# Gated attention and token mixer: the first layer's last pass as two passes of one block, and a shorter inner polynomial for gelu

## Chip, cores and metric

One core of one Trainium2 chip runs the whole kernel. The metric is device time in microseconds (us) of one launch.

## The reference

Input x is 2048 rows by 512 columns. Two branches are computed and mixed row by row:

```python
g = sigmoid((x * gate_w).sum(-1))
a = softmax attention of x, 32 heads of 16, then @ wo
h = layernorm(x)                                  # (2048, 512)
u = gelu(einsum("bsd,sf->bdf", h, w1) + b1)       # f = 1792: the first layer, over rows
y = einsum("bdf,fs->bds", u, w2) + b2             # the second layer, back to rows
out = g * a + (1 - g) * transpose(y)
```

gelu is the tanh form, 0.5 u (1 + tanh(0.798 (u + 0.0447 u^3))). The change touches the first layer of the second branch and its gelu.

## The kernel before

Values are kept as pairs of a high part (fp32r) and the low rest, so each product is three matmuls on TensorE (PE): high by high, high by low, low by high. To split a weight, ScalarE (ACT) copies the high part and GpSimd (POOL) subtracts it for the low part.

The work runs in stages: the values, keys and queries of attention are projected; then the first layer; then attention, in 128 parts, with the second layer and the late queries on PE beside it; then the output.

**The first layer.** The 1792 columns of w1 are taken in passes of up to NB = 512: four blocks of 128 columns in each of the first three passes, two blocks in the last (256 columns). Each pass runs over the 16 row blocks of x (`for at, c in enumerate(cs)`); a block has a PSUM bank of its own in which its 16 x 3 matmuls are added up (`layer`, L420). The last pass takes row blocks 8 to 15 first and 0 to 7 after (`order`, L126). The weights come through a queue, `blocks`: `load_weight` (L135) issues the next load into one of four raw tiles, `split_weight` (L149) splits the oldest that is loaded into one of three pairs of tiles `w_hi`, `w_lo`, and `weight` (L157) does both and hands out the oldest pair. Three pairs are split ahead of the loop, so a call of `weight` splits the weight three places on, whose tile is the one that the matmuls of this call's weight read. Behind the blocks of w1, the same queue holds those of w2: four 128 x 128 blocks in one tile.

**gelu.** `gelu` (L428) is a generator of seven steps for one block of 128 columns by 512: bias add on VectorE (DVE), Square on ACT, the inner polynomial on DVE (L437 and L438), tanh on ACT (L440), the outer product on DVE (L442), the high part on ACT (L444) and the low part on DVE (L446). The blocks of one pass go through it in the next pass. In the first and the last pass the order on ACT, DVE and POOL is written out by hand (`manual_schedule`): row block by row block, first the weight's split, then the steps that are due. In the last pass (L523) the four blocks of the pass before begin at row blocks 0, 1, 7 and 8, a step for each row block. In the two passes between, the compiler orders these engines.

**The last two blocks.** They have no pass behind them. Their bias add (L549, `late_u`) stands between the first layer and attention; the rest of their gelu lies in the first parts of attention, on DVE but for the tanh (L553 to L574): square (L555), the polynomial in two operations (L559, L563), tanh on ACT (L566), outer product (L570) and split. The tables `amid` and `later` say in which part, and whether ahead of the part's last two DVE copies or at its end.

**Attention.** A part computes 16 score tiles (L1067) of 128 x 512 on PE, each in a bank of its own while seven banks last. ACT takes ten of them out as exponentials (six single ones, L1093, and two pairs, L1031); DVE copies the other six (L1089), and ACT then takes the exponential of these six at once (L1102). PE applies them to the values (L963), with one or several matmuls of the dense layers beside the scores (L1076). All five engines have a written order here.

Of the kernel before, what the change touches and what calls it, by code (L numbers as in the profile page):

```python
# [13 lines left out]
AF = mybir.ActivationFunctionType  # L14
ALU = mybir.AluOpType
# [8 lines left out]
P = 128  # L24
S = 2048
D = 512
F = 1792
H = 32
DH = 16
NS = S // P  # L30
ND = D // P
NF = F // P
NB = 512
# [4 lines left out]
GELU_A = 0.044715  # L38
# [22 lines left out]
def gated_mix(ctx: ExitStack, tc: tile.TileContext, a_x, a_wqkv, a_wo, b_w1, b_b1, b_w2, b_b2, gate_w, out):  # L61
    nc = tc.nc
# [30 lines left out]
    g = const.tile([P, NS], F32, name="g")  # L93
# [23 lines left out]
    def bank():  # L117
        return acc.tile([P, NB], F32, name="acc")
# [4 lines left out]
    xt_lo = xt_pool.tile([P, ND, S], F32R, name="xt_lo")  # L123


    order = {f0: [(c + (NS // 2 if f0 + NB >= F else 0)) % NS for c in range(NS)] for f0 in range(0, F, NB)}  # L126
    blocks = [b_w1[c * P : (c + 1) * P, f0 : min(f0 + NB, F)] for f0 in order for c in order[f0]]
    blocks += [
        b_w2[c * P : min(c + 4, NF) * P, t * P : (t + 1) * P].rearrange("(k p) s -> p k s", p=P)
        for t in range(NS)  # L130
# [4 lines left out]
    def load_weight():  # L135
        if blocks:
            src = blocks.pop(0)
            raw = wk.tile([P, NB], F32, name="w_raw", bufs=4)
            if len(src.shape) == 2:
                raw = raw[:, : src.shape[1]]  # L140
                dst = raw
            else:
                raw = raw[:, : src.shape[1] * P]
                dst = raw.rearrange("p (k s) -> p k s", s=P)
            with tc.issue_after(x_load.ins):
                nc.sync.dma_start(dst, src)
            loaded.append(raw)
# [9 lines left out]
    def weight():  # L157
        load_weight()
        split_weight()
        return ready.pop(0)  # L160
# [17 lines left out]
    with tc.tile_pool(name="vp", bufs=1, side="right") as pool:  # L178
# [122 lines left out]
        for t in range(2, NS):  # L301
# [9 lines left out]
            ps = bank()  # L311
# [22 lines left out]
    h_hi, h_lo = {}, {}  # L334
# [15 lines left out]
    def ln_load(c):  # L350
        xs[c] = ln_x[:, c % 4, :]
        nc.sync.dma_start(xs[c], xf[c * P : (c + 1) * P, :])
# [10 lines left out]
    if True:  # L363
# [19 lines left out]
        for b in range(ND):  # L383
            wk_b, wq_b = qk_w.pop(0), qk_w.pop(0)
            kmax = bd.tile([P, NQ], F32, name="kmax")
            for at, (n, keys) in enumerate(jobs):
                ps = project(wk_b if keys else wq_b, n)
# [11 lines left out]
                if at in (2, 5):  # L399
                    c = 2 * b + at // 3  # L400
# [16 lines left out]
    u_hi = u_pool.tile([P, NF, D], F32R, name="u_hi")  # L417
    u_lo = u_pool.tile([P, NF, D], F32R, name="u_lo")

    def layer(ps, hi, lo, rhs, first, last):  # L420
        for i, p in list(enumerate(ps))[:: 1 if len(ps) == NB // P else -1]:
            wh, wl = hi[:, i * P : (i + 1) * P], lo[:, i * P : (i + 1) * P]
            for k, (a, b) in enumerate(((wh, rhs[0]), (wh, rhs[1]), (wl, rhs[0]))):
                nc.tensor.matmul(p, a, b, start=first and k == 0, stop=last and k == 2)  # L424

    with tc.tile_pool(name="gl", bufs=2, side="right") as gl:

        def gelu(ps, fb):  # L428

            u = gl.tile([P, D], F32, name="gu")  # L430
            s = gl.tile([P, D], F32, name="gs")
            hi, lo = u_hi[:, fb, :], u_lo[:, fb, :]
            nc.vector.tensor_scalar_add(u, ps, b1[:, fb : fb + 1])
            yield
            nc.scalar.activation(s, u, AF.Square)
            yield
            nc.vector.tensor_scalar(s, s, GELU_A, 1.0, ALU.mult, ALU.add)  # L437
            nc.vector.tensor_mul(s, s, u)  # L438
            yield
            nc.scalar.activation(s, s, AF.Tanh, scale=GELU_C)  # L440
            yield
            nc.vector.scalar_tensor_tensor(u, s, 1.0, u, ALU.add, ALU.mult)  # L442
            yield
            nc.scalar.copy(hi, u)  # L444
            yield
            nc.vector.tensor_tensor(lo, u, hi.bitcast(F32), ALU.subtract)  # L446
            yield

        beside = {mybir.EngineType.Activation, mybir.EngineType.DVE, mybir.EngineType.Pool}
        for c in range(AHEAD):  # L450
            ln_load(NH + c)


        def shift_rows(engine, t):
            for i in range(2):
                engine.memset(t[i * HALF + SHIFT[0] : i * HALF + SHIFT[0] + DH].bitcast(F32), -1.0)

        landed, waiting = [], []

        def stack(dst, src, which, pair, planes):  # L460
            b, r0 = divmod(pair * 2 * DH, P)
            for i in range(2):
                rows = slice(r0 + i * DH, r0 + (i + 1) * DH)
                for row, *part in planes:
                    at = slice(i * HALF + row, i * HALF + row + DH)
                    waiting.append((dst[at].bitcast(F32), src[b][part[which], rows, :]))

        def load_next():
            if waiting:
                landed.append(nc.sync.dma_start(*waiting.pop(0)))  # L470

        def load_all():
            while waiting:
                load_next()

        def load_k(g):
            t = k_bufs[g % 2]
            stack(t, kp_d, 1, g % NP, PAIRS)
            if g:
                load_all()  # L480
            return t

        def load_q(g):
            half, pair = divmod(g, NP)
            t = q_bufs[g % 2]
            stack(t, qp_d[half], 0, pair, [*PAIRS, SHIFT])
            if g:
                load_all()
            return t

        k_bufs, q_bufs = [], []

        def first_loads():
            k_bufs.append(first_stacks.tile([P, S], F32R, name="ks"))
            q_bufs.append(first_stacks.tile([P, QW], F32R, name="qs"))
            shift_rows(nc.vector, k_bufs[0])
            return {0: load_k(0)}, {0: load_q(0)}

        STEPS = 7
        gelus = []  # L500
        for f0, cs in order.items():
            n = min(NB, F - f0) // P
            ps = [bank() for _ in range(n)]
            in_order = f0 == 0 or f0 + NB >= F
            if f0 == NB:
                kt, qt = first_loads()
            if not in_order:
                for step in gelus:
                    list(step)
                gelus = []  # L510
            with tc.manual_schedule(engines=beside) if in_order else ExitStack():
                for at, c in enumerate(cs):
                    hi, lo = weight()

                    if f0 == 0 and AHEAD < c <= NH:
                        ln_load(NH + c - 1)
                    if f0 == 0 and AHEAD < c <= NH + AHEAD:
                        ln_rows(NH + c - AHEAD - 1)
                    layer(ps, hi, lo, (h_hi[c], h_lo[c]), at == 0, at == NS - 1)
                    if at % 2:  # L520
                        load_next()
                    for i, step in enumerate(gelus):
                        if 0 <= at - i // 2 * STEPS - i % 2 < STEPS:  # L523
                            next(step)
            gelus = [gelu(ps[i], f0 // P + i) for i in range(n)]
    h_ctx.close()


# [17 lines left out]
    for i, p in reversed(list(enumerate(ps))):  # L546
        u = out_pool.tile([P, D], F32, name="row", bufs=3)
        at = NF - len(ps) + i
# [136 lines left out]
    calls, later, amid = {}, {}, {}  # L685
# [4 lines left out]
    def on_dve(at, *what):  # L690
        later.setdefault(at, []).append(what)
# [161 lines left out]
            on_dve(2 * at + 2, *finish)  # L853
        return put(steps, at, [len(steps)])

    for i in range(2):
        on_dve(1 + i, tanh, i)
        on_dve(2 + i, outer_parts, i)
    for p, mid, what, i in (
        (0, True, squares, 0),  # L860
        (0, False, cubic, 0),
        (1, True, inner, 0),
        (1, False, squares, 1),
        (1, False, cubic, 1),
        (2, True, inner, 1),
        (2, False, outer, 0),
        (3, True, outer, 1),
    ):
        if mid:
            amid.setdefault(p, []).append((what, i))  # L870
        else:
            later.setdefault(p, []).insert(1 if what is cubic and i else 0, (what, i))
    call(3, load_xt, 2)
    for b in range(ND):
        call(6 + b, nc.sync.dma_start, v_d[b], vb[b][:, :BV])
    at, queries = 0, [(b, n) for n in (2, 3) for b in range(ND)]
    for t in range(NS):
        at = put(second_layer(t), at, [14] * 3)
        if queries:
            b, n = queries.pop(0)  # L880
            at = put_whole(late_query(b, n), at)
# [24 lines left out]
    for t in range(NH):  # L906
        at = put_whole(project(t), at)
# [82 lines left out]
    with tc.manual_schedule(engines=engines):  # L990
# [3 lines left out]
        for p in range(LAST + 1):  # L994
            grp, ph = divmod(p, PHASES)
            second = ph % 2
            if ph == 0:
                sums[grp] = ot_pool.tile([P, NB], F32, name="ot")
                latest["clear"] = nc.gpsimd.memset(sums[grp], 0.0)
                at = [[0, 0], [0, 0]]  # L1000
# [41 lines left out]
            for n in in_turn:  # L1042
                i, qb = head[n], qbs[n]
                c = at[i][qb]
                at[i][qb] += 1
                if n < TWO[0][0]:
                    if n >= BANKS:
                        ones[share[n - BANKS]] = psum.tile([P, NB], F32, name=f"s{share[n - BANKS]}")
                    s = ones[share[n % BANKS]]
                else:  # L1050
# [14 lines left out]
                    s = twos[share[2 if n == NSC - 1 else (n - BANKS) % BANKS]]  # L1065
# [8 lines left out]
                if n < n_b:  # L1074
                    ps, a, b, begin, last, done = beside[n]
# [72 lines left out]
    with (  # L1148
# [16 lines left out]
        sums, hi, lo = (column_halves(x) for x in (whole[:, :NB], parts[:, :NB], parts[:, NB:]))  # L1165
        last = column_halves(last_ot)
# [63 lines left out]
    with tc.If(far_off != 0):  # L1230
        with (
# [6 lines left out]
            for b in range(ND):  # L1238
                with tc.For_i(0, P // DH, 1) as hi:
# [11 lines left out]
                    for t in range(NS):  # L1251
                        s = ps_s.tile([P, S], F32, name="s")
# [6 lines left out]
                        p = pool.tile([P, S], F32, name="p", bufs=1)  # L1259
# [4 lines left out]
                        for n in range(NQ):  # L1264
                            tp = ps_t.tile([P, NB // P, P], F32, name="tp")
                            for i in range(NB // P):
                                c = n * (NB // P) + i
# [3 lines left out]
                            for i in range(NB // P):  # L1271
                                c = n * (NB // P) + i
# [38 lines left out]
```

## Time and profile before

| | us |
|---|---|
| median of 3 runs | 1265.4 (1265.24 to 1265.51) |
| the profiled execution | 1265.31 |
| its span, first to last instruction | 1263.5 |
| busy: PE, PE weight loads | 1254.8, 829.2 |
| busy: DVE, ACT, POOL | 856.7, 1069.0, 198.6 |
| the first layer's matmuls | 122.9 to 277.6 |

In the profile's lines, times are us from the start of the span. A line of the timeline gives start, duration, engine, line of the kernel, operation, what is written from what, shapes, and the count where several equal instructions follow each other; in brackets stands the engine's idle time before it and what ended that. "acc" is the first layer's bank, "gu" and "gs" are gelu's tiles, "row" and "big" those of the late blocks, "s", "t" and "u" score tiles, "p" and "pe" their exponentials. A line of the waits gives who waited for whom: us in total, times, longest. The mean granted clock of the span is 0.999.

### The profile page before, as it was taken

What the parts mean: (1) busy time and instruction counts of PE and PEld (TensorE: products, weight loads), DVE (VectorE), ACT (ScalarE), POOL (GpSimd) and SP (SyncE); (2) the same over time, 40 slices, a digit from 0 to 9 for tenths busy, and PEclk for the clock granted to TensorE, in tenths of its full rate; (3) what the DMA queues carried; (4) which work ended last, traced back from release to release, by engine and by line L of the source; (5) the groups of instructions that cost most, each with busy time, mean ns of one, the idle gap of its engine ahead of it and who ended that gap; (6) DMA issues with size and microseconds to landing.
All of it is one profiled execution on the core that took longest, in us unless ns stands there. A gap on an engine that the chain in (4) does not pass through costs nothing.

```text
span 1263.5 us, 32833 instructions
## 1 busy us (share of the span) xinstructions
PE 1254.8 (99%) x13342; PEld 829.2 (66%) x13342; DVE 856.7 (68%) x1562; ACT 1069.0 (85%) x1405; POOL 198.6 (16%) x316
## 2 busy tenths in 40 slices
PE   9999999999999999999999999999999999999998
PEld 7888888875666666666666666666666666666656
DVE  5675453178767676767677677776777677678883
ACT  4443343269999999999999999999999999999990
POOL 0220444461010101010110101111111111000000
PEclk9999999999999999999999999999999999999999
DMA  4799443244744444544344433444543443366611
GB/s 134 251 340 329 143 122 106 81 127 110 214 121 104 90 102 85 158 86 97 77 105 94 99 90 83 91 87 81 113 101 73 90 100 60 56 166 175 151 60 70
DMA packets 100556, 152.32 MB, mean 121 GB/s; under 512 B 17109, under 2 KB 56171, under 8 KB 96300
## 3 DMA queue, kind: packets, MB, share of 16 engines
q1 hardware_dynamic: 99820, 149.08, 46.0%
q8 instruction: 107, 1.75, 0.6%
q10 hardware_dynamic: 576, 1.05, 0.2%
q14 instruction: 53, 0.43, 0.1%
HBM read 105.39 MB, written 44.68 MB: 119 GB/s over the span
## 4 chain that ended last, share of the span: by engine, by line
PE 96%; DVE 2%; ACT 1%; issue 0%; DVEq 0%
PE av L963 31%; PE s L1067 21%; PE acc L424 12%; PE t L1067 9%; PE acc L75 8%; PE t L963 5%; PE dn L1076 3%; PE u L1067 3%; PE pa L1162 2%; DVE pe L1089 1%; PE acc L199 1%; PE acc L268 0%; DVE ot L985 0%; PE acc L245 0%; ACT p L1093 0%; ACT pe L1102 0%
## 5 line engine op out<-in xcount | busy, mean ns | idle before, releaser
L1093 ACT ACTIVATE p<-s 128x512 f32<-128x512 f32 x768 | 411.9, 789 | 0.1
L1102 ACT ACTIVATE pe<-pe 128x3072 f32<-128x3072 f32 x129 | 380.9, 2954 | 0.0
L1067 PE MATMUL s<-qs,ks 64*128 64x512 f32 x1280 | 329.8, 400 | 0.6 <-ACT p L1093 0.6
L1089 DVE COPY pe<-s 128x512 f32<-128x512 f32 x512 | 323.6, 685 | 5.5 <-PE s L1067 1.5
L1067 PEld LDWEIGHTS s<-qs,ks 64*128 64x128 f32 x1280 | 225.7, 184 | 92.7 <-issue 52.3
L1031 ACT ACTIVATE p<-t 128x1024 f32<-128x1024 f32 x256 | 278.7, 1267 | 0.0
L963 PE MATMUL av<-p,v 128*32 128x256 f32 x3880 | 227.2, 379 | 0.0
L1089 DVE COPY pe<-u 128x512 f32<-128x512 f32 x256 | 164.8, 685 | 67.1 <-PE u L1067 67.1
L963 PE MATMUL av<-pe,v 128*32 128x256 f32 x3072 | 192.5, 383 | 0.0
L985 DVE TENSOR_TENSOR ot<-av,ot 128x512 f32<-128x512 f32 (+2 forms) x160 | 93.0, 582 | 140.9 <-PE av L963 139.6
L68 POOL TENSOR_TENSOR w_lo<-w_raw,w_hi 128x512 fp32r<-128x512 f32 (+1 forms) x128 | 153.0, 1202 | 196.8 <-ACT w_hi L67 99.9
L1076 PE MATMUL dn<-u_lo,w_hi 64*128 64x512 f32 x448 | 181.0, 404 | 0.0
L1076 PE MATMUL dn<-u_hi,w_hi 64*128 64x512 f32 x448 | 180.7, 403 | 0.0
L963 PEld LDWEIGHTS av<-p,v 128*32 128x32 f32 x3880 | 126.0, 110 | 83.3 <-ACT p L1093 0.2
L1076 PE MATMUL dn<-u_hi,w_lo 64*128 64x512 f32 x448 | 180.6, 403 | 0.0
L1067 PE MATMUL t<-qs,ks 64*128 64x512 f32 x512 | 142.5, 413 | 0.0
L963 PEld LDWEIGHTS av<-pe,v 128*32 128x32 f32 x3072 | 86.8, 109 | 80.7 <-ACT p L1093 35.7
L1080 POOL MEMSET token<- 1x1 f32 x128 | 11.3, 88 | 742.7 <-PE dn L1076 679.4
L67 ACT CAST w_hi<-w_raw 128x512 fp32r<-128x512 f32 (+1 forms) x67 | 38.0, 569 | 82.7 <-PE acc L424 63.1
L1067 PEld LDWEIGHTS t<-qs,ks 64*128 64x128 f32 x512 | 73.2, 184 | 50.8 <-ACT p L1093 48.6
L424 PE MATMUL acc<-h_hi,w_hi 128*128 128x512 f32 x224 | 87.9, 392 | 0.0
L424 PE MATMUL acc<-h_hi,w_lo 128*128 128x512 f32 x224 | 87.9, 392 | 0.0
(171 smaller groups left out, 1615.8 us busy)
## 6 DMA issues: line engine op xcount, KB each, us to landing
w_raw<-in_B_w_dram SPq DMA_DIRECT2D x96, 256.0 KB
ks<-kp SPq DMA_DIRECT2D x192, 128.0 KB
qs<-qp SPq DMA_DIRECT2D x256, 64.0 KB
kp<-pc SPq DMA_DIRECT2D x16, 512.0 KB
qp<-pc SPq DMA_DIRECT2D x8, 768.0 KB
qp<-row SPq DMA_DIRECT2D x24, 256.0 KB
v<-v SPq DMA_DIRECT2D x4, 1088.0 KB
x<-in_A_x_dram SPq DMA_DIRECT2D x16, 256.0 KB
```

The lines of the kernel that those rows point to most:

```text
L67: copy(hi, src)
L68: return sub(lo, src, hi.bitcast(F32), ALU.subtract)
L75: nc.tensor.matmul(ps, a, b, start=start and n == 0, stop=stop and n == last)
L424: nc.tensor.matmul(p, a, b, start=first and k == 0, stop=last and k == 2)
L963: mm = nc.tensor.matmul(av[32 * j : 32 * (j + 1), i * QC : (i + 1) * QC], vb[b][:, v_at : v_at + 32], pt[:, h * QC : (h + 1) * QC], start= ...
L985: latest["add"] = nc.vector.tensor_tensor(x, y, x, ALU.add)
L1031: pairs_done.append(nc.scalar.activation(pt, twos[low, low + 1], AF.Exp, scale=SCALE))
L1067: nc.tensor.matmul(s, kt[grp][rows_i, c * P : (c + 1) * P], qt[grp][rows_i, qb * NB : (qb + 1) * NB], start=True, stop=True,)
L1076: mm = nc.tensor.matmul(ps, a[half], b[half], start=begin and not second, stop=last and bool(second))
L1089: nc.vector.tensor_copy(pt, s)
L1093: one = nc.scalar.activation(pt, s, AF.Exp, scale=SCALE)
L1102: done = nc.scalar.activation(x, x, AF.Exp, scale=SCALE)
```

## The change

- The last pass (two blocks) becomes two passes of one block each. A load of weights for these passes holds one block of 128 columns for four row blocks (128 x 512, in the form that w2's loads have), so `weight` is called for each fourth row block only.
- The blocks of the third pass go through gelu beginning at row blocks 0 and 7 of the first short pass and 0 and 8 of the second; the block of the first short pass itself begins at row block 4 of the second. One block, not two, is left for attention; its steps stand in parts 0 to 2.
- Square is scaled by the root of 0.0447, so that one DVE operation, (s + 1) u, replaces the two of the inner polynomial in the twelve, now thirteen, blocks that go through `gelu`.

```diff
+    starts = [0, NB, 2 * NB, F - 2 * P, F - P, F]
+    order = {f0: [(c + (NS // 2 if f0 + NB >= F else 0)) % NS for c in range(NS)] for f0 in starts[:-1]}
+    width = {f0: f1 - f0 for f0, f1 in zip(starts, starts[1:])}
+    blocks = [b_w1[c * P : (c + 1) * P, f0 : f0 + NB] for f0 in order if width[f0] == NB for c in order[f0]]
+    blocks += [
+        b_w1[c * P : (c + 4) * P, f0 : f0 + P].rearrange("(k p) s -> p k s", p=P)
+        for f0 in order
+        if width[f0] == P
+        for c in order[f0][::4]
+    ]
...
-    def layer(ps, hi, lo, rhs, first, last):
-        for i, p in list(enumerate(ps))[:: 1 if len(ps) == NB // P else -1]:
+    def layer(ps, hi, lo, rhs, first, last, n0=0):
+        for i, p in enumerate(ps, n0):
...
-            nc.scalar.activation(s, u, AF.Square)
+            nc.scalar.activation(s, u, AF.Square, scale=GELU_A**0.5)
             yield
-            nc.vector.tensor_scalar(s, s, GELU_A, 1.0, ALU.mult, ALU.add)
-            nc.vector.tensor_mul(s, s, u)
+            nc.vector.scalar_tensor_tensor(s, s, 1.0, u, ALU.add, ALU.mult)
...
-                    hi, lo = weight()
+                    if n > 1 or at % 4 == 0:
+                        hi, lo = weight()
...
-                    layer(ps, hi, lo, (h_hi[c], h_lo[c]), at == 0, at == NS - 1)
+                    layer(ps, hi, lo, (h_hi[c], h_lo[c]), at == 0, at == NS - 1, 0 if n > 1 else at % 4)
...
-                    for i, step in enumerate(gelus):
-                        if 0 <= at - i // 2 * STEPS - i % 2 < STEPS:
+                    for begin, step in gelus:
+                        if 0 <= at - begin < STEPS:
                             next(step)
-            gelus = [gelu(ps[i], f0 // P + i) for i in range(n)]
+            if f0 == F - 2 * P:
+                gelus = [(b - NS, g) for b, g in gelus if b >= NS] + [(4, gelu(ps[0], f0 // P))]
+                gelus.sort(key=lambda x: x[0])
+            else:
+                gelus = [(b, gelu(ps[i], f0 // P + i)) for i, b in zip(range(n), (0, 7, NS, NS + 8))]
...
+    amid[0] = [(squares, 0)]
+    on_dve(0, cubic, 0)
+    amid[1] = [(inner, 0)]
+    on_dve(1, tanh, 0)
+    on_dve(2, outer, 0)
+    on_dve(2, outer_parts, 0)
```

More of the change, by code (lines that the diff above doesn't have):

```diff
@@ L123, in gated_mix @@
     xt_lo = xt_pool.tile([P, ND, S], F32R, name="xt_lo")
-    order = {f0: [(c + (NS // 2 if f0 + NB >= F else 0)) % NS for c in range(NS)] for f0 in range(0, F, NB)}
-    blocks = [b_w1[c * P : (c + 1) * P, f0 : min(f0 + NB, F)] for f0 in order for c in order[f0]]
+    starts = [0, NB, 2 * NB, F - 2 * P, F - P, F]
[8 more added lines that the diff above has]
+    ]
     blocks += [
@@ L501, in gated_mix @@
         for f0, cs in order.items():
-            n = min(NB, F - f0) // P
+            n = width[f0] // P
             ps = [bank() for _ in range(n)]
@@ L507, in gated_mix @@
             if not in_order:
-                for step in gelus:
+                for _, step in gelus:
                     list(step)
@@ L854, in put_whole @@
         return put(steps, at, [len(steps)])
[L856 to L872, printed above, removed]
+    amid[0] = [(squares, 0)]
[4 more added lines that the diff above has]
+    on_dve(2, outer_parts, 0)
     call(3, load_xt, 2)
```

## The prediction

> **What bounds the kernel now.** I read the page first, then the chain of waits in order of time, then what ScalarE (ACT) waits for, then the timelines of ACT, VectorE (DVE) and GpSimd (POOL) around the end of the first layer. The page, ACT's busy tenths in 40 slices of the span, and the chain of waits by engine:
>
> ```profile
> ACT  4443343269999999999999999999999999999990
> ...
> PE 96%; DVE 2%; ACT 1%; issue 0%; DVEq 0%
> ```
>
> By the chain TensorE (PE) looks like the bound of the whole kernel; ACT is full only from the tenth slice on. The chain in order of time, and everything ACT waits for from 277 us to the end:
>
> ```profile
> 122.92 154.68 PE acc L424 x672
> 277.59 0.89 PE s L1067 x2
> 278.76 2.56 ACT p L1093 x5
> ...
> ACT o_sum L1210 <- PE pa L1192: 6.4, 1, 6.4
> ACT e L1180 <- DVE o_sum L1179: 5.2, 1, 5.2
> ACT w_hi L67 <- PE acc L424: 0.7, 1, 0.7
> ```
>
> Two stages with two bounds. The first layer is 672 matmuls in 154.68 us, 0.230 us apart, with no gap: PE bounds it, and the change keeps every one of these matmuls. From the first exponential on, ACT waits for nothing until the two lines of the closing stage (L1180, L1210): attention is one unbroken stream of ACT work. So each microsecond that ACT is given or spared there, and each microsecond by which its stream starts later, should move the end of the kernel by as much. The timeline of ACT:
>
> ```profile
> 277.45 0.62 ACT L67 CAST w_hi<-w_raw 128x512 fp32r<-128x512 f32 x1 [0.74 <-PE acc L424]
> 278.06 3.26 ACT L1093 ACTIVATE p<-s 128x512 f32<-128x512 f32 x6
> 281.16 1.99 ACT L1031 ACTIVATE p<-t 128x1024 f32<-128x1024 f32 x2
> 282.96 2.84 ACT L1102 ACTIVATE pe<-pe 128x3072 f32<-128x3072 f32 x1
> 285.63 3.11 ACT L1093 ACTIVATE p<-s 128x512 f32<-128x512 f32 x6
> ...
> 292.95 0.78 ACT L566 ACTIVATE big<-big 128x512 f32<-128x512 f32 x1
> 293.47 3.20 ACT L1093 ACTIVATE p<-s 128x512 f32<-128x512 f32 x6
> ...
> 308.77 3.24 ACT L1093 ACTIVATE p<-s 128x512 f32<-128x512 f32 x6
> ...
> 316.19 2.26 ACT L1093 ACTIVATE p<-s 128x512 f32<-128x512 f32 x4
> ```
>
> One of the 128 parts of attention is six single exponentials, two pairs and one wide one: 316.19 - 308.77 = 7.42 us when nothing is added. The late tanh of a block (L566; there are two, one a part later) takes a slot of 293.47 - 292.95 = 0.52 us, and the part that holds the first lasts from 285.63 to 293.47, 7.84 us. PE is done with the first layer at 277.45, where it releases the last weight buffer, and the first exponential starts 0.61 us later.
>
> **The change, part by part.** *PE.* The pass over 256 columns becomes two passes over 128, each with 16 x 3 matmuls. Two times 48 is 96 matmuls, as before; the last pass now fills only its second half, from about 277.45 - 11.05 = 266.4 us on. No change in PE time. *Weights.* Instead of 16 loads and splits of 128x256 there are 8 of 128x512. How these fit is seen in the pass before, which has the same 12 matmuls for one 128x512 load:
>
> ```profile
> 244.12 0.62 ACT L67 CAST w_hi<-w_raw 128x512 fp32r<-128x512 f32 x1 [2.18 <-PE acc L424]
> 246.92 0.62 ACT L67 CAST w_hi<-w_raw 128x512 fp32r<-128x512 f32 x1 [2.18 <-PE acc L424]
> ...
> 256.72 0.41 ACT L67 CAST w_hi<-w_raw 128x256 fp32r<-128x256 f32 x1 [0.99 <-PE acc L424]
> 258.12 0.41 ACT L67 CAST w_hi<-w_raw 128x256 fp32r<-128x256 f32 x1 [0.99 <-PE acc L424]
> 258.44 0.63 ACT L435 ACTIVATE gs<-gu 128x512 f32<-128x512 f32 x1
> ```
>
> ACT copies one weight each 246.92 - 244.12 = 2.80 us and idles 2.18 us of them "<-PE": supply is ahead, so larger loads cost PE nothing. If that cover went, a late weight would cost its lateness; none is near. But the rows tell a second thing. The copy is queued on ACT in program order, and it waits until PE has finished the weight three places earlier, whose buffer it takes. Whatever stands behind it on ACT waits too. Before, such a gate opened each 258.12 - 256.72 = 1.40 us, once for each row block, and the gelu steps of that row block stood right behind it (the Square at 258.44). After, it opens once for four row blocks, about each 2.8 us, and gelu steps of four row blocks bunch behind it. In the last pass, from 266.4 to 277.45, the gates open at about 269.2, 272.0, 274.7 and 277.4 us.
>
> *Gelu beside the last pass.* Three blocks must go through it in 11 us (starting at row blocks 0, 4 and 8), where before four went through in 22 us. Prices of the steps, and what DVE and POOL do to each other:
>
> ```profile
> 211.13 0.69 DVE L438 TENSOR_TENSOR gs<-gs,gu 128x512 f32<-128x512 f32 x1
> 212.20 1.66 DVE L438 TENSOR_TENSOR gs<-gs,gu 128x512 f32<-128x512 f32 x1
> 211.92 1.39 POOL L68 TENSOR_TENSOR w_lo<-w_raw,w_hi 128x512 fp32r<-128x512 f32 x1 [1.61 <-ACT w_hi L67]
> 266.74 0.53 POOL L999 MEMSET ot<- 128x512 f32 x1 [0.40 <-PE acc L424]
> 266.81 1.40 DVE L433 TENSOR_SCALAR gu<-acc,b 128x512 f32<-128x512 f32 x2
> ```
>
> A dependent ACT step is 0.63 us, a DVE step 0.69, the bias add 1.40/2 = 0.70. A DVE step that begins while POOL subtracts (212.20, POOL until 213.31) ends 0.55 us after POOL, at 213.86. I take that price: end of POOL plus 0.55. The Trainium skill, page "SBUF — State Buffer", section "Who interferes with whom", says that a DVE instruction with two SBUF inputs and a GpSimd instruction that reads SBUF exclude each other, and that the later one is fully blocked until the first is done. By that rule the blocked step would have ended at 213.31 + 0.69 = 214.0, and each of the blocked steps below would end 0.14 us later than by the row, some 0.5 us in all; the trace agrees with the blocking and is a little kinder, and the sum goes by the row.
>
> Followed from the first gate with these prices (an estimate): copy 269.2, Square 269.7 to 270.4, inner step blocked by POOL's subtraction (269.9 to 271.2) until 271.75, tanh until 272.4, outer step 273.1, add of the second block 273.8, its Square 274.45, low part of the first block behind POOL 275.0, inner 275.7, tanh 276.35, outer 277.05, add of the third block 277.75, its Square 278.35, low part of the second behind POOL 278.9, inner 279.6, tanh 280.25, outer 280.95, cast 281.6, low part up to 282.85 behind POOL's last subtraction. PE is through at 277.45. So on ACT a Square, a tanh, a weight copy and a cast, four slots of about 0.53 us, fall into attention, and on DVE two low parts, an inner and an outer step. Now what stands behind them:
>
> ```profile
> 277.19 1.40 DVE L549 TENSOR_SCALAR row<-acc,b 128x512 f32<-128x512 f32 x2
> 278.52 2.52 DVE L1089 COPY pe<-s 128x512 f32<-128x512 f32 x4
> 280.96 0.68 DVE L555 TENSOR_TENSOR big<-row 128x512 f32<-128x512 f32 x1
> 281.56 1.28 DVE L1089 COPY pe<-u 128x512 f32<-128x512 f32 x2
> ```
>
> The wide exponential of the first part started at 282.96 because DVE's last two copies ended at 281.56 + 1.28 = 282.84: DVE is already tight there. Before, DVE was free for its first copy at 278.52.
>
> If the queues keep the order of the program, the first exponential waits for the cast (281.55 instead of 278.06, +3.5) and DVE's copies for the low part (282.85 to 283.5 instead of 278.52): the wide exponential is 4.3 to 5.0 us late, and the rest of the stream with it. If the compiler mixes the tail with attention by readiness, DVE still owes from 277.75 on a blocked low part until 278.9, then inner, outer, low part (3 x 0.69) and the one late add (0.7): 281.65, 3.1 us past 278.52; POOL's last subtraction can add up to 0.7. The memset at 266.74, which belongs to attention and yet runs between the subtractions of the pass, shows that such mixing happens. What goes the other way: one late block instead of two, so one tanh, -0.52 us on ACT. The DVE steps of that block (square, inner, outer, split) and the shorter inner polynomial in earlier passes come out of DVE time behind which nobody waits: 0, a gain excluded by ACT's unbroken stream. If ACT weren't the bound there, it could be worth up to what the first four parts last over steady ones, (308.77 - 278.06) - 4 x 7.42 = 1.03 us with both tanh in it.
>
> Sum: +3.1 - 0.52 = +2.6 with mixing, +3.8 to +4.5 without. I take +3.0, nearer the mixed end because of that memset row. The profiled execution took 1265.31 us (span 1263.5 and 1.8 around it), 0.09 below the median of the runs, 1265.4: 1265.31 + 3.0 = **1268.3 us**.
>
> **Rivals.** *Order kept (strict queues).* 1265.31 + 3.8 to 4.5, about 1269.5 us. For it: both stages are written as ordered queues. Against it: the memset. It decides if DVE's first copy of attention stands behind the last low part.
>
> *A light tail.* POOL's subtractions happen not to meet the chain: without the four waits behind POOL (about 0.65, 0.5, 0.45 and 0.55 us in the steps above) the last block is through its low part at about 280.7 us. What then falls on DVE is an inner and outer step and a low part, 2.0 us, less 0.52: about 1266.8 us, within the bound of no change. For it: a few tenths in the start of a step decide whether it meets POOL. Against: POOL subtracts 1.4 of each 2.8 us.
>
> *The tail fits (the other side).* The chain of the third block ends before PE does, ACT's stream starts at 278.06 as before, and the spared tanh remains: 1265.31 - 0.52 = 1264.8 us, not slower. The place is the third block's low part, and the point is 277.45: the 17 dependent steps that follow the first gate, 269.2, would have to take under 0.49 us each. Against it: ACT alone takes 0.63, DVE 0.69. For it: only that the scheduler may place steps better than I follow them.
>
> *The blocks gain more than I see.* The change would have to save over 2.5 us of an ACT stream in which only 1.03 us is more than steady work; I find no row for it.
>
> **How the numbers follow.** Forecast 0.40, order kept 0.27, light tail 0.20, tail fits 0.08, more gain 0.05. About 0.2% (2.5 us) is what a measurement of this kernel can tell from no change, so the bound lies at 1267.9. The forecast's own spread, 1267.7 to 1269.0 for starts of steps that differ by some tenths, lies above it for about 0.33 of its 0.40: slower 0.33 + 0.27 = 0.60; same 0.07 + 0.20 + 0.08 = 0.35; faster 0.05. The range 1265.2 to 1270.2 leaves out the two gaining cases (0.13) and some 0.07 of later tails.
>
> **What would show it.** Right: matmuls of L424 still without a gap; gates on ACT 2.8 us apart; a Square, tanh and cast of the first layer's gelu after the last L424 matmul; the wide exponential of the first part starting about 3 us later against the first score matmul than 282.96 - 277.52 = 5.4; ACT's stream then unbroken at 7.42 us a part, and one L566 of 0.52 us. Its row for the score matmul:
>
> ```profile
> 277.52 0.50 PE L1067 MATMUL s<-qs,ks 64*128 64x512 f32 x1
> ```
>
> Wrong: gelu's last low part before 277.45, a gap among the L424 matmuls (then weights, not gelu, cost), a part other than the first one stretched, or a first part as long as before with the end later all the same.

## The result, and the profile after

| | before | after |
|---|---|---|
| median of 7 runs, us | 1265.44 | 1269.57 (1269.2 to 1269.82) |
| ratio, 95% interval | | 1.0031 [1.0019, 1.0042] |
| the profiled execution | 1265.31 | 1269.82 |
| its span | 1263.5 | 1267.9 |

The change costs 4.1 us, 0.31%; the interval of the ratio, 0.19 to 0.42%, reaches down to the prediction's bound of 0.2%. The time lies in the range that was forecast, 1265.2 to 1270.2, and 1.3 us above the forecast of 1268.3; what happened is the rival "order kept", about 1269.5. Three things in the profile after show it. The first is what PE waits for from another engine (us in total, times, longest):

```profile
PE s L1068 <- DVE row L561: 3.9, 1, 3.9
PE acc L253 <- DVE idle L248: 1.2, 1, 1.2
```

The second line stood in before too (L245 there). The first is new: one score matmul waits 3.9 us for the bias add of the late block (L561, `late_u`), which frees that block's PSUM bank. Timeline of PE, around the end of the first layer:

```profile
277.17 0.39 PE L432 MATMUL acc<-h_hi,w_lo 128*128 128x512 f32 x1
277.49 0.49 PE L1068 MATMUL s<-qs,ks 64*128 64x512 f32 x1
...
283.05 0.79 PE L1068 MATMUL s<-qs,ks 64*128 64x512 f32 x1 [3.90 <-DVE row L561]
283.64 0.62 PE L1068 MATMUL s<-qs,ks 64*128 64x512 f32 x1
```

The first score starts at 277.49, before at 277.52: PE's first layer has the same length. Six scores find free banks; the seventh has to take the bank of the block that has just been added up. Timeline of DVE after:

```profile
270.32 1.36 DVE L445 SCALAR_TENSOR_TENSOR gs<-gs,gu 128x512 f32<-128x512 f32 x1 [1.06 <-ACT gs L443]
...
279.77 0.69 DVE L449 SCALAR_TENSOR_TENSOR gu<-gs,gu 128x512 f32<-128x512 f32 x1 [0.69 <-ACT gs L447]
281.14 0.99 DVE L453 TENSOR_TENSOR u_lo<-gu,u_hi 128x512 fp32r<-128x512 f32 x1 [0.68 <-ACT u_hi L451]
282.24 0.75 DVE L561 TENSOR_SCALAR row<-acc,b 128x512 f32<-128x512 f32 x1
282.91 1.88 DVE L1090 COPY pe<-s 128x512 f32<-128x512 f32 x3
```

The late add's input was ready at 277.56 (277.17 + 0.39). It runs at 282.24, straight behind the last low part of the third block's gelu (L453). Its row shows no wait of its own: its place in DVE's queue keeps it. Attention's first copies (L1090) stand behind it, at 282.91, where before had them at 278.52. This is the second thing, and on ACT the same order stands:

```profile
269.13 0.62 ACT L67 CAST w_hi<-w_raw 128x512 fp32r<-128x512 f32 x1 [0.92 <-PE acc L432]
...
272.25 0.60 ACT L67 CAST w_hi<-w_raw 128x512 fp32r<-128x512 f32 x1
...
275.95 0.61 ACT L67 CAST w_hi<-w_raw 128x512 fp32r<-128x512 f32 x1
...
279.64 0.60 ACT L67 CAST w_hi<-w_raw 128x512 fp32r<-128x512 f32 x1
280.50 0.62 ACT L451 CAST u_hi<-gu 128x512 fp32r<-128x512 f32 x1 [0.25 <-DVE gu L449]
281.02 1.57 ACT L1094 ACTIVATE p<-s 128x512 f32<-128x512 f32 x3
...
288.67 2.77 ACT L1103 ACTIVATE pe<-pe 128x3072 f32<-128x3072 f32 x1 [0.73 <-DVE pe L1090]
...
298.67 0.69 ACT L578 ACTIVATE big<-big 128x512 f32<-128x512 f32 x1
...
313.89 3.24 ACT L1094 ACTIVATE p<-s 128x512 f32<-128x512 f32 x6
...
321.30 3.24 ACT L1094 ACTIVATE p<-s 128x512 f32<-128x512 f32 x6
```

The first exponential (281.02) is the first thing behind the last cast. The wide exponential of the first part is 5.71 us late (288.67 against 282.96). From 313.89 on, where before had 308.77, the stream is 5.12 us late at the same 7.41 us a part: 0.59 came back, with one tanh less.

The third thing shows in the windows. Columns: stretch, its length, busy us and count of PE, PEld, DVE, ACT and POOL, PE's granted clock (the share of full speed that PE was given), DMA share, GB/s:

```profile
277.00:279.00 2.00, 2.00 (x15) 1.19 (x13) 1.97 (x3) 1.06 (x2) 0.92 (x1) 1.00 0.58 164
279.00:283.00 4.00, 0.15 (x2) 0.00 (x0) 2.51 (x5) 3.23 (x6) 1.27 (x1) 0.92 1.06 205
283.00:289.00 6.00, 5.95 (x38) 3.73 (x42) 4.79 (x8) 3.84 (x6) 1.99 (x3) 0.50 0.62 82
289.00:291.00 2.00, 2.00 (x32) 1.06 (x26) 0.48 (x2) 2.00 (x1) 1.89 (x1) 0.95 0.00 0
```

After the wait PE runs at half its clock for about 6 us, while the copies and the wide exponential depend on its scores. From the late add to the wide exponential it takes 288.67 - 282.24 = 6.43 us, and from DVE's first copy 288.67 - 282.91 = 5.76 us, where before took 282.96 - 278.52 = 4.44 us.

At the other end of the kernel, the timelines of DVE in before and then in after, with the operation of the last output row:

```profile
1257.33 0.75 DVE L1205 SCALAR_TENSOR_TENSOR base<-pa,g,base 128x512 f32<-128x512 f32 x1 [2.03 <-PE pa L1162]
```

```profile
1262.53 0.75 DVE L1206 SCALAR_TENSOR_TENSOR base<-pa,g,base 128x512 f32<-128x512 f32 x1 [2.03 <-PE pa L1163]
```

The last operation ends 5.2 us later (1263.28 against 1258.08), the span only 4.4: what lies behind it (call it the closing time) fell from 5.4 to 4.6 us. So the sum of after, on the spans, is +4.39 (DVE's first copy, 282.91 against 278.52) + 1.32 (from there to the wide exponential) - 0.59 (one tanh) - 0.8 (closing time), about +4.4 with 0.1 of drift between.

### The profile page after: what moved, and what is told of

Same layout as the page of the kernel before. It is cut to its first block, busy times and chain, and to the rows that moved or that the text cites. A ratio compares the mean times of both kernels' runs of the same rounds, so it can differ in the third digit from the quotient of the medians.

```text
span 1267.9 us, 32773 instructions
## 1 busy us (share of the span) xinstructions
PE 1256.7 (99%) x13342; PEld 830.0 (65%) x13342; DVE 846.6 (67%) x1547; ACT 1069.2 (84%) x1399; POOL 194.4 (15%) x308
## 4 chain that ended last, share of the span: by engine, by line
PE 96%; DVE 3%; ACT 0%; issue 0%; ACTq 0%; DVEq 0%
PE av L964 31%; PE s L1068 21%; PE acc L432 12%; PE t L1068 8%; PE acc L75 8%; PE t L964 5%; PE dn L1077 4%; PE u L1068 3%; PE pa L1163 2%; DVE pe L1090 1%; PE acc L207 1%; PE acc L276 0%; DVE ot L986 0%; PE acc L253 0%; DVE u_lo L453 0%; DVE gs L445 0%
## 5 line engine op out<-in xcount | busy, mean ns | idle before, releaser
L1090 DVE COPY pe<-s 128x512 f32<-128x512 f32 x512 | 323.8, 686 | 4.8 <-PE dn L1077 1.1
L1090 DVE COPY pe<-u 128x512 f32<-128x512 f32 x256 | 164.9, 686 | 68.8 <-PE u L1068 68.7
L68 POOL TENSOR_TENSOR w_lo<-w_raw,w_hi 128x512 fp32r<-128x512 f32 x120 | 148.5, 1244 | 202.0 <-ACT w_hi L67 105.8
L67 ACT CAST w_hi<-w_raw 128x512 fp32r<-128x512 f32 x59 | 36.4, 619 | 80.0 <-PE acc L432 64.6
L432 PE MATMUL acc<-h_hi,w_hi 128*128 128x512 f32 x224 | 87.9, 393 | 0.0
L432 PE MATMUL acc<-h_hi,w_lo 128*128 128x512 f32 x224 | 87.9, 392 | 0.0
```

The lines of the kernel that those rows point to most:

```text
L67: copy(hi, src)
L68: return sub(lo, src, hi.bitcast(F32), ALU.subtract)
L1090: nc.vector.tensor_copy(pt, s)
```

## The experiments

The theory: in the queues of DVE and ACT the whole gelu tail stands ahead of attention; the late add, last in DVE's queue, holds the PSUM bank of PE's seventh score; and the wait halves PE's clock. Rivals: the number of late blocks or the weight loads set the time; the clock drop is a mere companion; and, for the small terms, attention itself became faster or slower.

All ratios are to before on the same chip, with a 95% interval; the median of before was 1265.37 to 1265.67 on the chips used. The columns show the late add's start, PE's wait for it, the wide exponential's shift against 282.96, and the closing time; these come from one profile of each kernel.

| kernel | median | ratio | late add | wait | shift | closing |
|---|---|---|---|---|---|---|
| before | 1265.44 | 1 | 277.19 | none | 0 | 5.4 |
| after | 1269.57 | 1.0031 [1.0019, 1.0042] | 282.24 | 3.9 | +5.71 | 4.6 |
| split_behind | 1265.37 | 0.9998 [0.9989, 1.0007] | 279.27 | 0.8 | +1.35 | 4.8 |
| spread | 1267.56 | 1.0015 [1.0006, 1.0024] | 280.36 | 2.2 | +3.57 | 4.7 |
| both | 1263.79 | 0.9986 [0.9977, 0.9995] | 277.79 | none | -0.06 | 4.6 |
| two_late | 1269.08 | 1.0029 [1.0018, 1.0041] | 280.10 | 3.0 | +4.42 | 4.7 |
| keep_busy | 1268.61 | 1.0024 [1.0015, 1.0033] | 282.22 | none | +4.30 | 4.8 |
| after_old_inner | 1272.32 | 1.0052 [1.0038, 1.0065] | 283.90 | 4.4 | +7.37 | 6.2 |
| before_inner | 1264.67 | 0.9994 [0.9985, 1.0003] | 277.11 | none | -0.08 | 4.7 |
| fifteen | 1271.15 | 1.0043 [1.0029, 1.0057] | 282.04 | 3.9 | +5.51 | 5.8 |
| before_inner_15 | 1265.62 | 1.0000 [0.9991, 1.0009] | 277.03 | none | -0.16 | 5.5 |
| both_15 | 1264.66 | 0.9993 [0.9984, 1.0002] | 277.87 | none | +0.03 | 5.9 |

**split_behind: the weight copy behind the gelu steps.** In the short passes the next weight is split after the steps of the fourth row block instead of ahead of those of the first.

```diff
-                    if n > 1 or at % 4 == 0:
+                    if n > 1:
                         hi, lo = weight()
+                    elif at % 4 == 0:
+                        load_weight()
+                        hi, lo = ready.pop(0)
...
+                    if n == 1 and at % 4 == 3:
+                        split_weight()
```

> The changed kernel, with the split of each four-row weight put behind the gelu steps of its row blocks on ACT instead of ahead of them. Theory (a chain of gelu steps, started late by the gate in front of it, ends after the first layer and holds the bank of the last block): the Square of the first block in the last pass moves from 269.7 to about 267.2 us, the last low part ends near 279.7 instead of 282.1, PE's wait ahead of the seventh score shrinks from 3.9 to about 1.4 us, and the time is 1266.3 to 1267.2. Rival (the amount of gelu work in the pass sets it, the gate does not matter): 1269.6, PE's wait still 3.9.

The median is 1265.37, below the 1266.3 to 1267.2 that were expected. The late add comes 3 us earlier, at 279.27, PE waits 0.8 us, and the clock after that wait stays whole (windows of split_behind, the stretch with the wait):

```profile
279.00:281.00 2.00, 1.18 (x10) 0.59 (x8) 1.89 (x4) 1.49 (x4) 1.29 (x1) 1.00 0.65 206
```

The place of the weight copies in ACT's queue, with the same work on every engine, moves the kernel by 4.2 us. That speaks for the theory, and against the weights as such. POOL's subtractions move along with the copies, but meeting them explains little: from 266.4 us on, the DVE steps that meet one take 1.9 us more than their usual 0.69 each in after and 1.3 us more in split_behind, and the late add comes 3.0 us earlier.

**spread: earlier begins for the third pass's blocks.** The first of the four is at 0, the others at 4, 8 and 16 instead of 7, 16 and 24, so two blocks instead of three are left for the last pass.

```diff
-                gelus = [... zip(range(n), (0, 7, NS, NS + 8))]
+                gelus = [... zip(range(n), (0, 4, 8, NS))]
```

> The changed kernel, with the third pass's blocks beginning at row blocks 0, 4 and 8 of the first short pass and 0 of the second (the first short pass's block still at 4). Same work, no gap between blocks. Theory: at the measured 3.7 us for a block the last low part ends at about 258.6 + 4 x 3.7 + 5.1 = 278.5, PE's wait falls under 0.5 us and the time is 1265.0 to 1265.9. Rival (loads of four row blocks or passes of one block cost PE or ACT time of their own): 1268 or more although the tail is gone.

It came out at 1267.56, some 1.7 us above what was expected. Two things were missed. First, the remaining chain still meets a copy and POOL's subtraction (timeline of DVE in spread: an inner step of 1.67 us; the late add at 280.36):

```profile
271.80 1.67 DVE L445 SCALAR_TENSOR_TENSOR gs<-gs,gu 128x512 f32<-128x512 f32 x1
...
280.36 0.75 DVE L561 TENSOR_SCALAR row<-acc,b 128x512 f32<-128x512 f32 x1
```

Second, the wait of 2.2 us sufficed to halve the clock (timeline of PE in spread, then its windows):

```profile
281.17 0.50 PE L1068 MATMUL s<-qs,ks 64*128 64x512 f32 x1 [2.20 <-DVE row L561]
```

```profile
283.00:285.00 2.00, 2.00 (x10) 1.11 (x8) 1.29 (x2) 1.41 (x3) 0.16 (x2) 0.50 1.03 127
```

From the late add to the wide exponential it takes 6.17 us here, and 5.04 in split_behind. Two of the eleven runs, the fastest (1266.65 and 1266.83), show a mean granted clock of 1.000; a drop like the profiled one, 3.41 us at half speed, would leave at most 0.9987. So this wait did not halve the clock in every run. A block less is worth less than the copies' place. As PE's wait did not fall under 0.5 us, the run does not decide against its rival; the next one does.

**both: the two edits together.**

> Both edits together: split behind the steps, and blocks at 0, 4, 8 and 0, 4. Theory: the last low part ends before PE is through with the first layer at 277.4; the attention stream starts as in the kernel before, with one tanh of 0.52 us less: 1264.9. Rival (late block work was never what the first parts waited for, or the passes cost something): 1265.4 or above.

This is the fastest kernel, 1.1 us below what was expected, and its interval lies below 1. The last low part (L453) starts at 275.21, before PE is done, and the late add waits for PE and not PE for it (timeline of DVE in both):

```profile
275.21 1.02 DVE L453 TENSOR_TENSOR u_lo<-gu,u_hi 128x512 fp32r<-128x512 f32 x1 [0.69 <-ACT u_hi L451]
277.79 0.75 DVE L566 TENSOR_SCALAR row<-acc,b 128x512 f32<-128x512 f32 x1 [1.56 <-PE acc L432]
```

And ACT in both, one exponential of the steady stream:

```profile
308.19 3.25 ACT L1099 ACTIVATE p<-s 128x512 f32<-128x512 f32 x6
```

The wide exponential stands where before had it, and the stream is 0.58 us ahead (308.19 against 308.77): the spared tanh, as expected. The span is 1.4 us shorter than that of before (1262.1); the closing time, which the expectation did not contain, makes up 0.8 of it. The closing time is tested below. With the queues in this order the mechanism of the rival "tail fits" is real.

**two_late: both blocks of the old last pass left for attention.** The two short passes stay, but the first one's block goes to attention too, as before the change.

```diff
-                gelus = [(b - NS, g) for b, g in gelus if b >= NS] + [(4, gelu(ps[0], f0 // P))]
-                gelus.sort(key=lambda x: x[0])
+                gelus = [(b - NS, g) for b, g in gelus if b >= NS]
+                left = ps
...
-    for i, p in reversed(list(enumerate(ps))):
+    ps = left + ps
+    for i, p in enumerate(ps):
```

The tables that place the late steps in attention's parts, not shown, are those of before.

> The changed kernel without the fifth gelu in the last pass: the first short pass's block is left to attention with the last one, as the kernel before does with its two. Four blocks begin at 0, 7 and 0, 8. Theory: the block that begins at row block 8 is still held by the gates at 274.7 and 277.4, its low part ends near 280.3, the bank is freed about 281 to 281.7 instead of 282.95; with a second tanh again 1268 to 1268.8. Rival (the fifth block alone is the cause): 1265.4.

It measured 1269.08, a little above the expectation, which had no clock in it (0.54 in 283 to 285). The tail is a block shorter, yet the late adds come only at 280.10 and there are two of them in front of the copies; PE waits 3.0 us. The tanh that is kept shows: the shift of the stream goes from +4.42 to +4.35 only, where after went from +5.71 to +5.12. So the block that the change takes out of attention is not what costs; the rest of the tail does. This run does not separate its copies from its blocks; split_behind and spread do.

**keep_busy: no idle PE.** Behind the sixth score of the first part, the same score matmul is run 17 times more into the same bank. This only repeats work.

```diff
+            for _ in range(17 if p == 0 and n == 5 else 0):
+                # the matmul above once more, into s
```

> The changed kernel, with the sixth score matmul of attention's first part issued 17 more times (same operands, same bank), so that PE works through most of the 3.9 us in which it waited for the last block's bank. Theory (after the wait the granted clock is 0.50, and that makes the next scores and value matmuls take 0.42 instead of 0.23 us each): clock near 1.0 in this stage, the first wide exponential about 1.5 to 2.5 us earlier than 288.7, time 1267.2 to 1268.2 in spite of the added matmuls. Rival (the slow matmuls come from loads or from what ACT and DVE do then): 1269.6 or more.

The late add stays where it was (282.22), PE is busy in place of the wait, and the clock is whole (timeline of PE in keep_busy: 14 of the 17, and the seventh score; then its windows; then DVE's first copies):

```profile
278.94 3.35 PE L1076 MATMUL s<-qs,ks 64*128 64x512 f32 x14
283.02 0.49 PE L1068 MATMUL s<-qs,ks 64*128 64x512 f32 x1
```

```profile
279.00:283.00 4.00, 3.97 (x19) 2.89 (x17) 2.50 (x5) 3.23 (x6) 1.29 (x1) 1.00 1.09 207
283.00:289.00 6.00, 5.98 (x66) 3.55 (x68) 5.45 (x10) 5.18 (x6) 3.21 (x3) 1.00 0.60 81
```

```profile
282.89 2.47 DVE L1098 COPY pe<-s 128x512 f32<-128x512 f32 x4
```

The wide exponential comes 1.41 us earlier than in after and 5.04 us after the late add. The median falls by 1.0, less than expected (1.4 to 2.4). The clock drop is thus a cost of its own of 1.0 to 1.4 us. The rest, +4.30 at the wide exponential, is the lateness of DVE's queue: with a whole clock the wide exponential comes 287.26 - 282.89 = 4.37 us after DVE's first copy, in before 4.44. So PE's wait costs nothing here beyond the clock, since DVE's copies stand behind the tail as well. No run moves the late add alone ahead of the tail; by these numbers it would spare the clock drop and leave the copies late.

**after_old_inner and before_inner: the shorter polynomial by itself.** One puts the two operations back into after, the other puts the one operation into before.

```diff
-            nc.scalar.activation(s, u, AF.Square, scale=GELU_A**0.5)
+            nc.scalar.activation(s, u, AF.Square)
...
-            nc.vector.scalar_tensor_tensor(s, s, 1.0, u, ALU.add, ALU.mult)
+            nc.vector.tensor_scalar(s, s, GELU_A, 1.0, ALU.mult, ALU.add)
+            nc.vector.tensor_mul(s, s, u)
```

> The changed kernel with the old inner polynomial in two DVE operations. Theory: the polynomial lies in the chain of the three blocks, so each block gets about 0.45 us longer and the last low part ends 1.3 to 2 us later: 1270.8 to 1271.8. Rival (DVE's number of operations lies beside other work): 1269.6.

> The kernel before with the one-operation inner polynomial alone. Theory: its gelu steps end ahead of the first layer in any case, so nothing moves: 1265.4, within 0.3. Rival (the polynomial matters by itself): 0.5 us or more either way.

In after the old form costs 2.75 us by the medians, more than expected, and 3.3 by the spans (1271.2 against 1267.9): the tail's chain grows by 1.66 us (late add 283.90 against 282.24), and 1.6 lie in the closing time, 6.2 us against 4.6. PE waits twice there, 0.9 us for the third block's bias add and 4.4 us for the late add. In before the new form, by the median, gains 0.8 us where nothing was expected; the interval, 0.9985 to 1.0003, still holds no change. Its first part and its stream stand as in before (-0.08, -0.07); the closing time fell from 5.4 to 4.7.

**fifteen, before_inner_15, both_15: as many DVE instructions as before.** The closing times so far went with the number of DVE instructions in the program: 4.6 to 4.8 us with 1547 to 1550 of them, 5.4 and 6.2 with 1562 and 1560. These three add 15 memsets of a small tile, deep in attention: fifteen adds them to after, all in part 64; the other two add one in each of the parts 64 to 78, to before_inner and to both.

```diff
+        for _ in range(15 if p == 64 else 0):    # fifteen
+            nc.vector.memset(mark, 0.0)
...
+        if 64 <= p < 79:                         # before_inner_15, both_15
+            nc.vector.memset(mark, 0.0)
```

> The changed kernel with 15 one-element memsets on DVE in part 64 of attention, so that DVE's program is as long as in the kernel before. The stream of attention ends 5.2 us later than before, yet the time is only 4.1 us longer: what follows the last row sent out takes 4.6 us instead of 5.4. Theory (where DVE's program ends decides a last fetch of instructions): 0.8 us more, about 1270.4, and 5.4 us again after the last row. Rival (that closing time differs by chance or by something else): 1269.6.

> The kernel before with the one-operation inner polynomial, and 15 one-element memsets on DVE, one in each of parts 64 to 78 of attention, so that DVE's program is about as long as before again. Theory (the 0.7 us that the polynomial alone saved lie behind the last row sent out and come from a DVE program that needs one fetch of instructions fewer there): the closing time goes from 4.65 back to 5.4 us or more, 1265.2 to 1266.0. Rival (the polynomial itself saves it in the passes): 1264.7, closing time 4.65.

> The version with the split behind the steps and the blocks at 0, 4, 8 and 0, 4, with the same 15 memsets. Theory: of its 1.6 us some 0.55 are the tanh that attention no longer does and stay, some 0.9 come from the shorter DVE program and go: 1264.6 to 1265.2, wide exponentials still 0.55 us earlier than in the kernel before. Rival (all of the gain is gelu work): 1263.8.

Against before on the same chip, the medians rise by 1.6 us (fifteen), 0.7 (before_inner_15) and 0.6 (both_15), and the closing time by 1.2, 0.8 and 1.3. Fifteen came out above its 1270.4, the other two as expected; both_15 keeps its stream 0.5 us ahead, but its interval reaches 1: of the 1.6 us that both gained, 0.6 went again with the closing time. In fifteen another 0.3 us arise in the stream behind part 64. The last row's DVE operation in fifteen:

```profile
1262.77 0.75 DVE L1208 SCALAR_TENSOR_TENSOR base<-pa,g,base 128x512 f32<-128x512 f32 x1 [2.03 <-PE pa L1165]
```

The last row's operation ends within 0.3 us of that in after, and the span is 1.4 longer (1269.3 against 1267.9). So the closing time follows the length of DVE's program: shown, by adding and by removing. Where it is lost shows in the trace's records of semaphore instructions, which no view lists. In the closing time all engines wait for each other, and POOL releases the other four through one semaphore (97). In the seven kernels with the short closing time DVE takes it within 0.01 us of PE; in the five with the long one it does so 1.0 to 1.6 us after PE (in before at 1263.19 against 1262.21), and then the others wait for DVE. What holds DVE up there is open. That it is the loading of its instructions is a guess; the counts of the packets of instruction queue q14 don't settle it (53 in before, 52 in after_old_inner, although both have the long closing time).

## Where the prediction was right, and where it failed

- **PE: no change.** Right. The first layer ends where it did and its matmuls have no new wait.
- **The weights cost PE nothing.** Right, no matmul of L432 waits for one.
- **Gates 2.8 us apart.** Half right. The first opened as followed, at 269.13 (forecast 269.2). The next copies ran at 272.25, 275.95 and 279.64, 3.1 us and then twice 3.7 apart: they stand in ACT's queue behind a tanh that was itself late, so copy and chain held each other up. That the copies' place is the dear thing is shown by split_behind.
- **The chain of the third block.** Right to within 0.7 us. The last cast ran from 280.50 to 281.12 (followed: 281.0 to 281.6), the last low part ended at 282.13 (followed: 282.85). The first inner step, which meets POOL, ended at 271.68 (followed: 271.75). The low parts that met POOL took 0.99 to 1.02 us and ended 0.54 us after its subtraction (the price taken was 0.55).
- **Strict or mixed order.** This is the step that failed. The forecast has DVE's first copy 3.1 us late, by mixing; it came 4.39 us late, behind the whole tail. With strict order the prediction itself gave 4.3 to 5.0 us; it took +3.1 since the memset on POOL seemed to show mixing. POOL's timeline after has the same memset between two subtractions, while ACT and DVE keep the order:

```profile
269.83 1.30 POOL L68 TENSOR_TENSOR w_lo<-w_raw,w_hi 128x512 fp32r<-128x512 f32 x1 [1.12 <-ACT w_hi L67]
272.15 0.53 POOL L1000 MEMSET ot<- 128x512 f32 x1 [1.02 <-PE acc L432]
272.93 1.30 POOL L68 TENSOR_TENSOR w_lo<-w_raw,w_hi 128x512 fp32r<-128x512 f32 x1 [0.25 <-ACT w_hi L67]
```

  Here the memset on POOL said nothing about the queues of the other two. Both stages have their order written out, and that should have weighed more.
- **The shift of the wide exponential, 4.3 to 5.0 with strict order.** DVE's first copy is 4.39 us late, as followed. What was missing is PE: the late add is also what frees the seventh bank, so PE stops for 3.9 us and comes back at half its clock. That is 1.32 us more, 1.41 by keep_busy, and the shift became 5.71.
- **One tanh, -0.52.** Right: the shift fell by 0.59 in after and by 0.52 in both (from -0.06 to -0.58).
- **The shorter polynomial, 0.** Wrong in a small way: 15 DVE instructions fewer than in before take 0.8 us off the closing time. That no term had it at all is the second gap in the sum. The two misses, +1.3 and -0.8, nearly cancel, and so the time of the strict rival, 1269.5, came out almost to the tenth; part of that was luck.

The light tail did not occur, and the tail fits only where the copies stand behind the steps and the blocks begin earlier.

## What to carry to other kernels

When work of one stage is moved to the end of another, look for the operation behind it in the same queue that frees a buffer for the next stage: here one 0.75 us add, 4.7 us late, stopped PE and halved its clock, 1.3 us. Look also at what else stands behind the moved work: the next stage's first copies came 4.4 us late, more than all that the change saved. Put a copy that waits for a buffer behind the steps that are ready, not ahead of them, and begin the steps so early that the last one is done before the stage's last matmul. If two queues have a written order, forecast with that order, and do not take one operation of a third engine as evidence of mixing.

## What the runs showed of the hardware

PE's clock fell to 0.50 with waits of 3.9 us (after) and of 2.2 us (the profiled run of spread), and stayed at 1.00 after one of 0.8 us (split_behind). It was back some 6 us after PE resumed in after (0.95 in 289 to 291). The Trainium skill, page "TensorE: Matmul & The Clock Gate", section "Part 1: The HAM clock gate (the "warmup" mystery)", has two states, half and full rate, with the half one after at least one idle window of about 3.4 us. The two values agree; the length does not hold as a threshold for a wait here, since the 2.2 us in spread were enough. The trace's clock records show a length of this size in another way: the clock changes in steps. Where it fell at this place it had been whole for 276.48 us in all five kernels, which is 81 times 3.413 us, and it was then half for one such step (3.41 us: spread, two_late) or for two (6.83 us: after, after_old_inner, fifteen). In the last step before the drop PE was idle for 3.2 of the 3.41 us in after, and for 2.2 in spread. That a wait counts by how much of one such step it fills is an inference from these five traces; it would fit the two runs of spread whose clock did not fall.

The closing time, from the last output row's DVE operation to the end of the span, was 4.6 to 4.8 us in the seven kernels with 1547 to 1550 DVE instructions and 5.4 to 6.2 us in the five with 1560 to 1565, whatever the other work was. In the long cases DVE takes POOL's release 1.0 to 1.6 us after PE does. Why is open.
